# Attention into a gated MLP on one core: GpSimd's order, the sinks' keys, beta's turns and the fillers of the opening

## The chip, the cores and the metric

The kernel runs on one core of one Trainium2 chip. The metric is the device time of one execution in microseconds, median over runs. TensorE (PE) multiplies, ScalarE (ACT) evaluates exp and tanh, VectorE (DVE) masks, normalises and gates, GpSimd (POOL) casts, makes masks and issues transfers, SyncE (SP) issues transfers.

## The reference

```
attention: scores = q k^T / 8 over 768 positions, D = 64, 4 batches x 8 heads
           kept where k_pos < 4 (sinks) or 0 <= q_pos - k_pos < 128; softmax; times v
x    = attention output as [3072 tokens, 512]
h    = x @ w_in            (512 x 2048)
g    = h * sigmoid(beta*h) (beta: one value for each of the 2048 columns)
out  = g @ w_out           (2048 x 512), float32
```

## The kernel before

The 3072 tokens are eight tiles of 384 (half of a batch's 768 positions). Attention works on 32 units: a unit `n` is one tile and one pair of heads, four units to a tile. For a unit, q and k are cast to bf16, turned by TensorE (`transpose_first` for the first four, `transpose_in` for eight more, a transposing transfer for the rest), multiplied to scores, exponentiated by ScalarE into `E`, multiplied with v and a column of ones (`attend`), divided by VectorE (`normalise`) into `o_norm`, and turned again into `xT`. The first four units have their window mask added on TensorE: two products of `ident` with `add_mask` (the mask preloads, L711) stand ahead of each half of a unit's scores (L722).

Then, for each tile, 16 hidden blocks `h = w_in^T xT` (L836, four products each), tanh on ScalarE (L844, scaled by `beta_half`), the gate on VectorE (L857), and the output products with `w_out` (L865), interleaved with the attention of later tiles.

`Prog` is a planner. `op` records operations with what they read and write; `order` and `round` place them engine by engine from estimated costs; `emit` writes each engine's program in that order, with a semaphore wait wherever a dependency is not already implied. `after=[...]` adds a dependency that is only there to hold an operation back; between two operations of one engine it can become a wait of the engine for its own earlier instruction. `seq="name"` puts operations of one list into a fixed order without a semaphore. The planner also sets fillers on TensorE: until the hidden products of the first tile, it puts products of ones with ones (L461, into `acc[0]`, which nobody reads then) into a gap that it foresees, 0.8 of the gap less 60 ns, with a filler's cost doubled before `WARM` = 7000 ns.

The loads of the opening: SyncE issues q and k of the first four units, each 192 KB (`load_qk`), ScalarE issues beta and the first v (`load_v32`). GpSimd casts k and v (`cast`, L634; `cast_v`, L543) and issues w_in in four parts (`load_w_in`, L590); the first four keys of each head, the sinks, come by two small transfers from GpSimd's queue that also cast them to bf16 (`load_sinks(1, ...)`, L605, into `k_rows`), are turned by `sink_keys` (L617) and copied into `k_sink`. SyncE's second round of q and k (units 4 to 7) is held until w_in's second part has landed. beta arrives as 16 rows of 128; four fp32 turns on TensorE (L941) and four small VectorE operations (L946) make `beta_half`, just ahead of the last turns into `xT`.

Of the kernel before, what the change touches and what calls it, by code (L numbers as in the profile page):

```python
# [106 lines left out]
class Prog:  # L107
# [13 lines left out]
    QUEUE = {"sp": 1200.0, "act": 1200.0, "gp": 2100.0}  # L121
    TAIL, MIX, HEAVY, RING = 900.0, 1.1, 2.5, 8

    WARM, SWITCH = 7000.0, 95.0

    def __init__(self):
        self.nodes = []
# [114 lines left out]
    def round(self, took, freed):  # L242
        for n in self.nodes:
            n.open, n.place, n.ready = len(n.preds), None, 0.0
        free = dict.fromkeys(self.ENGINES, self.BEGIN)
        left = {e: [n for n in self.nodes if n.eng == e] for e in self.ENGINES}
        head = dict.fromkeys(self.ENGINES, 0)
        can = {e: [n for n in left[e] if n.open == 0] for e in self.ENGINES}
        issued = dict.fromkeys(self.ENGINES, 0)
        mode = 128  # L250
        placed = []

        def best(e):
# [12 lines left out]
            n = min(c, key=lambda n: (at[n.id], n.id))  # L266
            return at[n.id], n

        while any(n.place is None for n in self.nodes):
            found = [(*b, e) for e in self.ENGINES if (b := best(e)) is not None]  # L270
            start, n, e = min(found, key=lambda f: (f[0], f[1].id))
            busy = n.busy
            if e == "pe":
                if self.filler is not None and self.fill_until.place is None:
                    fn, cost, (source, _) = self.filler
                    at = max(free[e], source.done) if source.place is not None else start
                    cost *= 2.0 if at < self.WARM else 1.0
                    for _ in range(int((start - at - 60.0) * 0.8 / cost)):
                        f = Node(-1, "pe")
                        f.items.append((fn, None, [self.filler[2]]))  # L280
                        f.place = at
                        placed.append(f)
                        at += cost
                if n.mode != mode:
                    start, mode = start + self.SWITCH, n.mode
                if start < self.WARM:
                    busy *= 2.0
            free[e] = start + busy
            if n.dma is None:
                n.done = start + busy + n.lag  # L290
            else:
                n.done = start + took.get(n.id, busy + n.work + 3000.0)
                issued[e] += 1
            n.place = start
            can[e].remove(n)
            placed.append(n)
            for s in n.succs:
                s.open -= 1
                soft = n.id not in s.hard or (s.eng == e and n.dma is None)
                s.ready = max(s.ready, start + busy if soft else n.done)  # L300
                if s.open == 0:
                    can[s.eng].append(s)
        return placed
# [64 lines left out]
def bass_streamingllm_window__then__act_swish_beta_kernel(  # L368
# [45 lines left out]
    qk16 = [sb(f"qk16_{z}", (128, 2, 3, 2, D), BF16) for z in range(NQK)]  # L414
    v_aug = sb("v_aug", (128, 4, 2, 7, D + 2), BF16)
    v_sink = sb("v_sink", (128, NPAIR, 2, D1), BF16)
    k_rows = sb("k_rows", (NPAIR, NSINK, 2, D), BF16)
    k_sink = sb("k_sink", (128, NPAIR, 128), BF16)
    qkT = [sb(f"qkT{z}", (128, 2, 2, TT), BF16) for z in range(4)]
    E = [sb(f"E{z}", (128, 2, 768), BF16) for z in range(NE)]  # L420
# [121 lines left out]
    def cast_v(n):  # L542
        op("gp", lambda e: e.tensor_copy(v_aug[:, n, :, 0:3, 0:D].rearrange("p h c d -> p c h d"),  # L543
                                         v_stage[:, :, 2 * n:2 * n + 2, :]),
           r=[("v_stage", n // 2, c) for c in range(3)],
           w=[("v", n, kb, hh) for kb in range(3) for hh in range(2)], busy=460.0, lag=100.0)

    def load_v(T, c, after=()):

# [35 lines left out]
    w_in_src = moe_w_in.rearrange("(c p) f -> p c f", p=128)  # L585
    w_out_src = moe_w_out.rearrange("(g p j) n -> p g j n", p=128, j=PER)

    def load_w_in(m, ms, after=()):
        here = slice(m * 128, (m + ms) * 128)
        op("gp", lambda e: e.dma_start(w_in16[:, :, here], w_in_src[:, :, here]), after=after,  # L590
           w=[("w_in", c, mm) for c in range(4) for mm in range(m, m + ms)],
           dma=f"wi{m}", late=0.0 if m else 800.0, **transfer(DM * ms * 128 * 4, 385, 740.0, 3.0))

# [6 lines left out]
    def load_sinks(x, after=()):  # L600
        for hh in range(2):
            rows = slice(HEAD1 * hh, HEAD1 * hh + NSINK)
            if x:
                src = k[:, :, 0:NSINK, :].rearrange("b (g h) s d -> h (b g) s d", h=2)[hh]
                op("gp", lambda e, hh=hh, src=src: e.dma_start(k_rows[:, :, hh, :], src),  # L605
                   w=[("k_rows", hh)], after=after, dma=f"sk{hh}", busy=650.0, lag=300.0, weight=0.4)
            else:
                src = v[:, :, 0:NSINK, :].rearrange("b (g h) s d -> s h (b g) d", h=2)[:, hh]
                op("gp", lambda e, rows=rows, hh=hh, src=src: e.dma_start(v_sink[rows, :, hh, 0:D], src),
                   w=[("v_sink", hh)], r=["v_sink"], after=after, dma=f"sv{hh}", busy=650.0, lag=400.0, weight=0.4)  # L610

    def sink_keys():

        bank16 = tr_ps[:, :].bitcast(BF16)
        with P.together("pe"):
            for s in range(NSINK):
                op("pe", lambda e, s=s: nc.tensor.transpose(  # L617
                    bank16[:, s * NPAIR:(s + 1) * NPAIR],
                    k_rows[:, s, :, :].rearrange("n h d -> n (h d)"), ident[0:NPAIR, 0:NPAIR]),
                   r=[("k_rows", 0), ("k_rows", 1), "ident"], w=["tr"], **pe(60))  # L620
        src = bank16[:, 0:NSINK * NPAIR].rearrange("x (s n) -> x n s", s=NSINK)
        for hh in range(2):
            rows = slice(64 * hh, 64 * hh + 64)
            op("act", lambda e, hh=hh, rows=rows: e.copy(
                k_sink[rows, :, HEAD1 * hh:HEAD1 * hh + NSINK], src[rows]),
               x=["tr"], r=["k_sink"], w=[("k_sink", hh)], **act(100))

    def cast(n):
        _, _, half, pb = place(n)
        z = n % NQK  # L630
        here = slice(3 * half, 3 * half + 3)
        for x, name in enumerate("qk"):
            eng = "dve" if n < 4 and x == 0 else "gp"
            op(eng, lambda e, x=x, name=name, eng=eng: (e.copy if eng == "act" else e.tensor_copy)(  # L634
                qk16[z][:, x, :, :, :], stage[name][pb][:, :, here, :].rearrange("p h c d -> p c h d")),
               r=[(name + "_stage", pb, half)], w=[(name + "16", z)],
               **(dve(300.0) if eng == "dve" else {"busy": 460.0, "lag": 100.0}))

    def aside(n, step):
# [248 lines left out]
    for n in range(4):  # L888
        for x in range(2):
            load_qk(n, x)  # L890
    for c in range(6):
        load_v32(c // 3, c % 3)
    op("act", lambda e: e.activation(scratch[:, :], ones32[:, 0:1], AF.Exp, bias=0.0, scale=1.0),
# [1 line left out]
    cast(0)  # L895
    cast(1)
    cast_v(0)
    load_w_in(0, 4, [("v", 0, 0, 0)])
    cast_v(1)
    cast(2)  # L900
    load_sinks(1, [("v", 1, 0, 0)])

    select(ident32[:, :], ones32[:, :], [[1, 32]], ALU.is_equal, 0.0, 0, -1, ["ones32"], ["ident32"])
    transpose_first(0)
# [4 lines left out]
            scores(n, c, pairs[c])  # L909

    transpose_first(1)
    first_scores(0)
    cast(3)
    load_w_in(4, 4, [("k16", 0)])
    cast_v(2)
    load_w_in(8, 4, [("v", 2, 0, 0)])
    cast_v(3)
    load_w_in(12, 4, [("v", 3, 0, 0)])
    for n in range(4):
        if n < 2:  # L920
            transpose_first(n + 2)
        if n < 3:
            first_scores(n + 1)
        if n == 2:
# [5 lines left out]
            load_sinks(0, [("v", 3, 0, 0)])  # L930
# [8 lines left out]
    with P.together("pe"):  # L939
# [4 lines left out]
    with P.together("dve"):  # L944
        for y in range(PER):
# [1 line left out]
                beta_half[32 * y:32 * y + 32, :].rearrange("p (g j) -> p j g", j=PER),  # L947
                acc[1][0:32, 0:PER * NM].rearrange("p (j g y) -> p j g y", j=PER, y=PER)[:, :, :, y],
                0.5, None, ALU.mult),
               x=["acc1"], w=["beta"], **dve(100.0))  # L950
# [124 lines left out]
```

## Time and profile before

| | us |
|---|---|
| median of 3 runs (226.69 to 227.7) | 226.96 |
| the profiled execution | 228.2 |
| its span, first to last instruction | 226.5 |
| PE busy | 220.2 |
| ACT busy | 140.8 |
| DVE busy | 132.4 |
| POOL busy | 123.7 |

A busy PE counts pipelined matmuls whose ends are modelled. In the lists below, a row has its start, its length, the engine, the line, the operation, and in brackets how long the engine had been idle before it and what ended that. PEld is TensorE's weight load, and an engine with a q behind it (SPq, POOLq) is its issuing of transfers. In the chain of work in order of time a row is start, length, engine, tile and line. q0 is the transfer queue that GpSimd's issues go to, q1 SyncE's, q10 ScalarE's.

### The profile page before, as it was taken

The page shows a single profiled execution, that of the slowest core. Times are in us where ns is not written, and L with a number is a line of the kernel's source. Part 1 is how long each engine was busy: PE and PEld are TensorE (multiplying, and loading weights), DVE is VectorE, ACT ScalarE, POOL GpSimd, SP SyncE. Part 2 cuts the span into 40 slices and gives each one's busy share as a digit, 9 for nine tenths or more (in the row PEclk, how much of TensorE's full clock was granted, in tenths as well). Part 3 has the DMA queues.
Part 4 walks back from the last instruction along what each step waited for, and adds up shares of the span by engine and source line. Part 5 has one row for each costly group of instructions (what it writes and reads, how often), then busy time and mean ns, then how long its engine had stood idle before and what let it go on. Part 6 is the DMA issues. An engine that isn't in the chain of part 4 may idle for free.

```text
span 226.5 us, 4467 instructions
## 1 busy us (share of the span) xinstructions
PE 220.2 (97%) x1764; PEld 131.2 (58%) x1764; DVE 132.4 (58%) x263; ACT 140.8 (62%) x220; POOL 123.7 (55%) x191
## 2 busy tenths in 40 slices
PE   7999988999999999999999999999999999999995
PEld 4557654565666565555555555555565555555554
DVE  5447887549886666656565555566566555443300
ACT  1576887349576687656776766656676773555410
POOL 4589791989967969793939578694500000000000
PEclk9999999999999999999999999999999999999999
DMA  6999999999999999999999999999912202111022
GB/s 173 252 157 159 263 213 209 252 223 162 143 140 77 117 145 158 136 135 145 127 106 133 132 110 147 129 101 162 124 36 64 67 17 64 49 46 46 13 82 93
DMA packets 95877, 28.92 MB, mean 128 GB/s; under 512 B 83424, under 2 KB 91888, under 8 KB 95856
## 3 DMA queue, kind: packets, MB, share of 16 engines
q0 software_dynamic: 58208, 10.92, 61.5%
q1 hardware_dynamic: 34304, 16.79, 32.7%
q10 hardware_dynamic: 3344, 0.93, 1.9%
q8 instruction: 14, 0.23, 0.4%
q14 instruction: 7, 0.06, 0.1%
HBM read 27.34 MB, written 6.29 MB: 148 GB/s over the span
## 4 chain that ended last, share of the span: by engine, by line
PE 92%; ACT 3%; DMA 2%; SPq 0%; DVE 0%; issue 0%; ACTq 0%
PE acc L865 36%; PE h_ps L836 34%; PE s_ps L749 5%; PE s_ps L792 4%; DMA q_stage<-in_q_dram 2%; PE acc L836 2%; PE h_ps L865 2%; PE acc L792 1%; ACT E L729 1%; PE s_ps L781 1%; PE s_ps L692 1%; PE acc L461 1%; PE s_ps L711 1%; PE s_ps L722 1%; PE s_ps L674 1%; ACT th L844 1%
## 5 line engine op out<-in xcount | busy, mean ns | idle before, releaser
L844 ACT ACTIVATE th<-h_ps,beta_half 128x384 f32<-128x384 f32 x120 | 69.1, 581 | 53.0 <-PE h_ps L836 52.1
L865 PE MATMUL acc<-w_out,g 128*128 128x512 bf16 x368 | 99.4, 380 | 0.0
L836 PE MATMUL h_ps<-xT,w_in 128*128 128x384 bf16 x480 | 96.1, 326 | 0.0
L857 DVE SCALAR_TENSOR_TENSOR g<-th,h_ps 128x384 bf16<-128x384 f32 x120 | 65.5, 550 | 45.0 <-ACT th L844 44.3
L836 PEld LDWEIGHTS h_ps<-xT,w_in 128*128 128x128 bf16 x480 | 53.0, 113 | 33.7 <-DVE g L857 1.0
L865 PEld LDWEIGHTS acc<-w_out,g 128*128 128x128 bf16 x368 | 33.0, 98 | 27.9 <-issue 3.5
L564 POOL DMA_DIRECT2D land<-in_q_dram x40 | 30.2, 760 | 24.5 <-DVE rden L801 24.4
L757 ACT ACTIVATE E<-s_ps 128x1536 bf16<-128x1536 f32 x24 | 34.7, 1444 | 2.2 <-PE s_ps L749 2.1
L763 DVE TENSOR_TENSOR E<-E,mask 128x1536 bf16<-128x1536 bf16 x24 | 23.0, 957 | 15.8 <-ACT E L757 15.7
L564 POOL DMA_DIRECT2D land<-in_k_dram x40 | 30.3, 761 | 0.0
L573 POOL DMA_DIRECT2D v_aug<-in_v_dram x40 | 30.3, 761 | 0.0
L873 ACT ACTIVATE out_sb<-acc 128x512 f32<-128x512 f32 x23 | 13.7, 598 | 12.0 <-PE acc L865 11.8
L792 PEld LDWEIGHTS s_ps<-v_aug,E 128*128 128x128 bf16 x288 | 13.2, 97 | 2.9 <-issue 1.3
L792 PE MATMUL s_ps<-v_aug,E 128*128 128x65 bf16 x288 | 14.6, 193 | 0.0
L803 DVE TENSOR_TENSOR o_norm<-s_ps,rden 128x384 bf16<-128x384 f32 x24 | 13.3, 556 | 0.8
L749 PE MATMUL s_ps<-qkT 64*128 64x128 bf16 (+2 forms) x168 | 12.1, 257 | 0.0
L749 PEld LDWEIGHTS s_ps<-qkT 64*128 64x128 bf16 x168 | 5.7, 94 | 8.2 <-issue 6.2
L729 ACT ACTIVATE E<-s_ps 128x768 bf16<-128x768 f32 x9 | 7.3, 822 | 4.9 <-PE s_ps L722 4.9
L781 PE MATMUL s_ps<-v_sink,E_sink 128*128 128x130 bf16 x48 | 9.3, 219 | 0.0
L634 POOL CAST qk<-k_stage 128x384 bf16<-128x384 f32 x12 | 6.2, 513 | 5.2 <-DMA k_stage<-in_k_dram 5.2
L695 ACT ACTIVATE E_sink<-s_ps 128x384 bf16<-128x384 f32 x16 | 7.9, 493 | 0.8 <-PE s_ps L692 0.8
L554 POOL DMA_DIRECT2D v_aug<-in_v_dram x6 | 5.3, 898 | 5.1 <-DMA w_out<-in_moe_w_out_dram 5.1
(81 smaller groups left out, 159.6 us busy)
## 6 DMA issues: line engine op xcount, KB each, us to landing
out_dram<-out_sb SPq DMA_DIRECT2D x23, 256.0 KB, 2.4
q_stage<-in_q_dram SPq DMA_DIRECT2D x12, 192.0 KB, 6.9
k_stage<-in_k_dram SPq DMA_DIRECT2D x12, 192.0 KB, 7.2
w_in<-in_moe_w_in_dram POOLq DMA_DIRECT2D x4, 512.0 KB, 8.4
w_out<-in_moe_w_out_dram POOLq DMA_DIRECT2D x8, 256.0 KB, 8.8
land<-in_q_dram POOLq DMA_DIRECT2D x40, 48.0 KB, 3.1
land<-in_k_dram POOLq DMA_DIRECT2D x40, 48.0 KB, 3.6
v_aug<-in_v_dram POOLq DMA_DIRECT2D x40, 48.0 KB, 3.5
```

What stands on the lines that cost most here:

```text
L564: op("gp", lambda e, d=d, s=s: e.dma_start(d, s), w=[("land", pb, half, x, hh)], after=after, late=1800.0, dma=f"l{pb}{half}{x}{hh}", **tr ...
L573: op("gp", lambda e, d=d, s=s: e.dma_start(d, s), w=[("v", pb, 3 * half + c, hh) for c in range(3)], after=after, dma=f"lv{pb}{half}{hh}", ...
L749: op("pe", lambda e, at=at, w=w, kb=kb, qb=qb, nq=nq, hh=hh, rows=rows, bank=bank: e.matmul(s_ps[:, 2 * hh + bank, at:at + w], keys_of(pb, ...
L757: op("act", lambda e: e.activation(E[z][:, :, :], src, AF.Exp, bias=0.0, scale=SCALE), x=list(S_NAMES), w=[("E", z, 0), ("E", z, 1)], **ac ...
L763: op("dve", lambda e: e.tensor_tensor(E[z][:, :, :], E[z][:, :, :], m.unsqueeze(1).to_broadcast([128, 2, 768]), ALU.mult), r=[("E", z, 0), ...
L792: last=(x == len(kbs) - 1): e.matmul(av_ps[:, at + hh * D1:at + hh * D1 + D1], E[z][:, hh, col:col + 128], v_aug[:, pb, hh, column(n, kb), ...
L803: op("dve", lambda e: e.tensor_tensor(o_norm[o][:, :, :, :].rearrange("p m h d -> p (m h) d"), src[:, :, 0:D], rden[z][:, :].unsqueeze(2). ...
L836: op("pe", lambda e: e.matmul(bank, w_in16[:, c, m // PER * 512 + m % PER:m // PER * 512 + 512:PER], xT[:, c, T * TT:(T + 1) * TT], start= ...
L844: op("act", lambda e: e.activation(th[i % 3][:, :], bank, AF.Tanh, bias=0.0, scale=beta_half[:, m:m + 1]), x=[name], r=["beta"], w=[("th", ...
L857: op("dve", lambda e: e.scalar_tensor_tensor(g[T % 2][:, m, :], th[i % 3][:, :], 1.0, bank, ALU.add, ALU.mult), r=[("th", i % 3)], x=[name ...
L865: op("pe", lambda e: e.matmul(bank[:, 0:width], g[T % 2][:, m, t * 128:(t + 1) * 128], w_out16[:, m, cols], start=(m == 0), stop=(m == NM ...
L873: op("act", lambda e: e.activation(out_sb[z][:, 0:width], bank[:, 0:width], AF.Copy, bias=0.0, scale=0.5), x=[name], w=[("out_sb", z)], ** ...
```

## The change

- GpSimd: the casts of the first four units, the casts of v and the four issues of w_in are put on one list (`seq="loads gp"`), and the `after` that held w_in's parts behind casts goes. The third k is cast ahead of the second v.
- The sinks' keys: `k_rows` becomes fp32 and is loaded by two issues on SyncE, behind its first eight; `sink_keys` turns fp32 with `ident32`.
- beta's turns are recorded ahead of the first scores, and VectorE's part of it behind the cast of unit 1's q. In the resulting order TensorE's four turns stand right behind the first fillers, ahead of the first mask preloads.
- The fillers' rule has three stages: before 7 us the whole gap, to 10 us 0.8 of the gap less 60 ns at 1.5 times the cost, later half of the gap less 200 ns; the count is rounded at 0.7. TensorE's fillers in order are 14, 3, 5, 3, 7, 1, 2, 2, 3, 1, 7 before and 18, 3, 8, 2, 5, 1, 3 after.

Since the planner places everything anew, other instructions move too: between about 35 and 60 us some scores and output products on TensorE change places; the first is the second half of unit 7's scores, which goes from ahead of the first output products to behind the eighth.

```diff
-    WARM, SWITCH = 7000.0, 95.0
+    WARM, SURE, SWITCH = 7000.0, 10000.0, 95.0
...
-                    cost *= 2.0 if at < self.WARM else 1.0
-                    for _ in range(int((start - at - 60.0) * 0.8 / cost)):
+                    cost *= 2.0 if at < self.WARM else 1.5 if at < self.SURE else 1.0
+                    gap = start - at if at < self.WARM else 0.8 * (start - at - 60.0) if at < self.SURE else 0.5 * (start - at - 200.0)
+                    for _ in range(int(gap / cost + 0.3)):
...
-    k_rows = sb("k_rows", (NPAIR, NSINK, 2, D), BF16)
+    k_rows = sb("k_rows", (NPAIR, NSINK, 2, D), F32)
...  cast_v:
-           w=[("v", n, kb, hh) for kb in range(3) for hh in range(2)], busy=460.0, lag=100.0)
+           w=[("v", n, kb, hh) for kb in range(3) for hh in range(2)], busy=460.0, lag=100.0, seq="loads gp")
...  load_w_in:
-        op("gp", lambda e: e.dma_start(w_in16[:, :, here], w_in_src[:, :, here]), after=after,
+        op("gp", lambda e: e.dma_start(w_in16[:, :, here], w_in_src[:, :, here]), seq="loads gp",
...
+    def load_sink_keys():
+        for hh in range(2):
+            src = k[:, :, 0:NSINK, :].rearrange("b (g h) s d -> h (b g) s d", h=2)[hh]
+            op("sp", lambda e, hh=hh, src=src: e.dma_start(k_rows[:, :, hh, :], src),
+               w=[("k_rows", hh)], dma=f"sk{hh}", seq="loads sp", busy=520.0, lag=150.0, weight=0.4)
...  sink_keys:
-                    k_rows[:, s, :, :].rearrange("n h d -> n (h d)"), ident[0:NPAIR, 0:NPAIR]),
+                    k_rows[:, s, :, :].rearrange("n h d -> n (h d)"), ident32[0:NPAIR, 0:NPAIR]),
...  cast:
+               seq="loads gp" if eng == "gp" and n < 4 else None,
...  main program:
+    load_sink_keys()
...
-    load_w_in(0, 4, [("v", 0, 0, 0)])
-    cast_v(1)
-    cast(2)
-    load_sinks(1, [("v", 1, 0, 0)])
+    load_w_in(0, 4)
+    cast(2)
+    cast_v(1)
...  moved from behind the loop over the first four units to ahead of first_scores(0):
+    with P.together("pe"):
+        for j in range(PER):
+            op("pe", ... nc.tensor.transpose(acc[1][0:32, j * NM:(j + 1) * NM], beta_stage[:, j:128:PER], ident32[0:NM, 0:NM]) ...)
+    with P.together("dve"):
+        for y in range(PER):
+            op("dve", ... x=["acc1"], w=["beta"], after=[("q16", 1)], **dve(100.0))
...
-    load_w_in(4, 4, [("k16", 0)])
+    load_w_in(4, 4)
-    load_w_in(8, 4, [("v", 2, 0, 0)])
+    load_w_in(8, 4)
-    load_w_in(12, 4, [("v", 3, 0, 0)])
+    load_w_in(12, 4)
```

More of the change, by code (lines that the diff above doesn't have):

```diff
@@ L586, in bass_streamingllm_window__then__act_swish_beta_kernel, with load_w_in @@
     w_out_src = moe_w_out.rearrange("(g p j) n -> p g j n", p=128, j=PER)
-    def load_w_in(m, ms, after=()):
+    def load_w_in(m, ms):
         here = slice(m * 128, (m + ms) * 128)
-        op("gp", lambda e: e.dma_start(w_in16[:, :, here], w_in_src[:, :, here]), after=after,
+        op("gp", lambda e: e.dma_start(w_in16[:, :, here], w_in_src[:, :, here]), seq="loads gp",
            w=[("w_in", c, mm) for c in range(4) for mm in range(m, m + ms)],
@@ L598, in load_w_out, with load_sinks @@
            dma=f"wo{m}", **transfer(ms * 128 * NOUT * 4, 416, 740.0, 3.0))
-    def load_sinks(x, after=()):
+    def load_sink_keys():
[3 more added lines that the diff above has]
+               w=[("k_rows", hh)], dma=f"sk{hh}", seq="loads sp", busy=520.0, lag=150.0, weight=0.4)
+    def load_sinks(after=()):
         for hh in range(2):
             rows = slice(HEAD1 * hh, HEAD1 * hh + NSINK)
[L603 to L610, printed above, removed]
+            src = v[:, :, 0:NSINK, :].rearrange("b (g h) s d -> s h (b g) d", h=2)[:, hh]
+            op("gp", lambda e, rows=rows, hh=hh, src=src: e.dma_start(v_sink[rows, :, hh, 0:D], src),
+               w=[("v_sink", hh)], r=["v_sink"], after=after, dma=f"sv{hh}", busy=650.0, lag=400.0, weight=0.4)
     def sink_keys():
-        bank16 = tr_ps[:, :].bitcast(BF16)
         with P.together("pe"):
@@ L617, in sink_keys @@
                 op("pe", lambda e, s=s: nc.tensor.transpose(
-                    bank16[:, s * NPAIR:(s + 1) * NPAIR],
-                    k_rows[:, s, :, :].rearrange("n h d -> n (h d)"), ident[0:NPAIR, 0:NPAIR]),
-                   r=[("k_rows", 0), ("k_rows", 1), "ident"], w=["tr"], **pe(60))
-        src = bank16[:, 0:NSINK * NPAIR].rearrange("x (s n) -> x n s", s=NSINK)
+                    tr_ps[:, s * NPAIR:(s + 1) * NPAIR],
+                    k_rows[:, s, :, :].rearrange("n h d -> n (h d)"), ident32[0:NPAIR, 0:NPAIR]),
+                   r=[("k_rows", 0), ("k_rows", 1), "ident32"], w=["tr"], **pe(60))
+        src = tr_ps[:, 0:NSINK * NPAIR].rearrange("x (s n) -> x n s", s=NSINK)
         for hh in range(2):
@@ L911, in bass_streamingllm_window__then__act_swish_beta_kernel @@
     transpose_first(1)
+    with P.together("pe"):
+        for j in range(PER):
+            op("pe", lambda e, j=j: nc.tensor.transpose(acc[1][0:32, j * NM:(j + 1) * NM], beta_stage[:, j:128:PER],
+                                                        ident32[0:NM, 0:NM]),
+               r=["beta_stage", "ident32"], w=["acc1"], **pe(64))
+    with P.together("dve"):
+        for y in range(PER):
+            op("dve", lambda e, y=y: e.tensor_scalar(
+                beta_half[32 * y:32 * y + 32, :].rearrange("p (g j) -> p j g", j=PER),
+                acc[1][0:32, 0:PER * NM].rearrange("p (j g y) -> p j g y", j=PER, y=PER)[:, :, :, y],
+                0.5, None, ALU.mult),
+               x=["acc1"], w=["beta"], after=[("q16", 1)], **dve(100.0))
     first_scores(0)
     cast(3)
-    load_w_in(4, 4, [("k16", 0)])
+    load_w_in(4, 4)
     cast_v(2)
-    load_w_in(8, 4, [("v", 2, 0, 0)])
+    load_w_in(8, 4)
     cast_v(3)
-    load_w_in(12, 4, [("v", 3, 0, 0)])
+    load_w_in(12, 4)
     for n in range(4):
@@ L929, in bass_streamingllm_window__then__act_swish_beta_kernel @@
             masks([("v", 3, 0, 0)])
[L930 removed]
+            load_sinks([("v", 3, 0, 0)])
             for c in range(3):
@@ L936, in bass_streamingllm_window__then__act_swish_beta_kernel @@
         normalise(n, *bank)
-    with P.together("pe"):
-        for j in range(PER):
-            op("pe", lambda e, j=j: nc.tensor.transpose(acc[1][0:32, j * NM:(j + 1) * NM], beta_stage[:, j:128:PER],
-                                                        ident32[0:NM, 0:NM]),
-               r=["beta_stage", "ident32"], w=["acc1"], **pe(64))
-    with P.together("dve"):
-        for y in range(PER):
-            op("dve", lambda e, y=y: e.tensor_scalar(
[L947 to L950, printed above, removed]
     for n in range(4):
```

## The prediction

> **What bounds the kernel now.** I read the page's 40 slices first, then its chain of work that ended last, then that chain in order of time for 0 to 60 us.
>
> ```profile
> PE   7999988999999999999999999999999999999995
> PEclk9999999999999999999999999999999999999999
> PE 92%; ACT 3%; DMA 2%; SPq 0%; DVE 0%; issue 0%; ACTq 0%
> 8.29 0.43 PE acc L461 x3
> 8.72 0.32 PE s_ps L674 x3
> 9.04 0.64 PE s_ps L711 x2
> 9.68 0.75 PE acc L461 x7
> 12.94 0.33 PE s_ps L711 x2
> 15.23 0.11 PE acc L461 x2
> 17.61 0.17 PE acc L461 x3
> 18.44 0.14 PE acc L941 x4
> 18.91 0.39 PE acc L461 x7
> 19.30 0.26 PE s_ps L820 x3
> 19.55 0.49 PE h_ps L836 x3
> 28.24 0.34 PE s_ps L656 x3
> 36.24 0.34 PE h_ps L722 x4
> 36.58 0.97 PE acc L865 x4
> 38.42 0.86 PE acc L865 x4
> ```
>
> TensorE (PE) carries 92% of the chain, and from 37 us on nothing else stands in it. The work behind that point is the same in both kernels, so this case is decided by what TensorE loses before. It loses at three places: the opening up to the first hidden product at 19.55, the turns of the second round of q and k at 28.24, and the stretch before 36.24, where ScalarE paces.
>
> Two more things are in these rows. The L461 rows are fillers: products of ones that nobody reads, put where the planner expects TensorE to wait. They are on the chain themselves, so a filler in the wrong place delays the work behind it. And two mask preloads took 0.64 us at 9.04 but 0.33 us at 12.94: TensorE worked at half rate until about 12.8 us, although the granted clock reads full in every slice.
>
> **The fillers.** In the changed program's order the first gaps get 18, 3 and 8 fillers instead of 14, 3 and 5; the next two get 2 and 5 instead of 3 and 7; all later ones together get 4 instead of 16.
>
> ```profile
> 1.16 1.68 PE L461 MATMUL acc<-ones 128*128 128x128 bf16 x14 [1.16 <-DVE ones L455]
> 4.71 0.50 PE L674 MATMUL s_ps<-ident,qk 128*128 128x128 bf16 x3 [0.47 <-DVE qk L634]
> 4.94 0.51 POOL L634 CAST qk<-k_stage 128x384 bf16<-128x384 f32 x1 [1.98 <-DMA k_stage<-in_k_dram]
> 6.75 0.50 PE L722 MATMUL s_ps<-qkT 64*128 64x384 bf16 x2 [0.21 <-DVE qkT L681]
> 16.14 1.51 ACT L729 ACTIVATE E<-s_ps 128x768 bf16<-128x768 f32 x2 [0.16 <-PE s_ps L722]
> 18.52 0.56 DVE L803 TENSOR_TENSOR o_norm<-h_ps,rden 128x384 bf16<-128x384 f32 x1
> ```
>
> A cold filler costs 0.75 / 7 = 0.107 us. The 18 first ones end at 1.16 + 18 x 0.107 = 3.09. Then come beta's four turns (0.14 at full rate, up to 4 x 0.107 = 0.43 cold) and four preloads at 0.32 each, together 1.28: 4.5 to 4.8 against the 4.71 at which q's first turn starts anyway. A slip of 0.1 would end at the next wait, because k's turn needs the cast that ends at 4.94 + 0.51 = 5.45. The eight fillers behind it start at about 5.82 (k's turn at 5.50 plus 0.32) and end at 6.68, before the scores at 6.75. The added fillers are hidden, by hundredths.
>
> The removed ones are worth more. From 8.29 to 12.94 the chain is TensorE alone, without a wait, so three cold fillers fewer there bring 3 x 0.107 = 0.32. Behind 12.94 TensorE and ScalarE's exponentials release each other in turn, which keeps this lead but adds little. The last exponential ends at 16.14 + 1.51 = 17.65, and three fillers stand in front of the product that waits for it (17.61); one is left, which brings 2 x 0.056 = 0.11. The last turn needs o_norm, ready at 18.52 + 0.56 = 19.08, and starts at 19.30 behind seven fillers; three are left, and of these 0.22 us I take 0.1 (the rest is the hop between the engines). Sum of the opening: 0.53. Its bounds are 0, if the exponentials and copies were late by themselves, and 1.0, if every filler from 12.94 on counted: 12 fewer at 0.056 are 0.67 beside the 0.32.
>
> **Beta's turns.**
>
> ```profile
> 0.81 0.43 ACTq L886 DMA_DIRECT2D beta_stage<-in_moe_beta_dram  x1
> beta_stage<-in_moe_beta_dram ACTq DMA_DIRECT2D x1, 8.0 KB, 2.2
> 9.08 0.56 DVE L681 COPY qkT<-s_ps 128x384 bf16<-128x384 bf16 x1 [1.79 <-PE s_ps L674]
> 19.00 0.73 DVE L946 TENSOR_SCALAR beta_half<-acc 32x16 f32<-32x16 f32 x4
> ```
>
> They leave 0.14 us of TensorE at 18.44 and 0.73 us of VectorE at 19.00. At 18.44 TensorE was early for o_norm anyway. VectorE's work, ending at 19.73, held the last xT copy by 0.2 us (its turn ended at 19.30 + 0.26), and six hidden products at 0.49 / 3 each, 19.55 to 20.53, cover that copy. So this brings nothing. In the new place VectorE's 0.73 lies in an idle 1.79 us ahead of 9.08; without that cover it would cost its 0.73. TensorE's four turns add a wait for beta's transfer, landing at 0.81 + 2.2 = 3.01, just ahead of the 3.09 at which they are reached. The preloads and q's first turn are queued behind it, with VectorE and ScalarE waiting for them; a landing up to 0.3 later would be swallowed, and each us beyond costs at most one. I take 0.
>
> **GpSimd's waits and the sinks' keys.**
>
> ```profile
> POOL w_in L590 <- POOL v_aug L543: 0.9, 3, 0.3
> 11.00 1.02 POOL L605 DMA_DIRECT2D k_rows<-in_k_dram  x2
> 12.82 0.76 POOL L590 DMA_DIRECT2D w_in<-in_moe_w_in_dram  x1 [0.30 <-POOL qk L634]
> 4.62 0.47 SPq L533 DMA_DIRECT2D k_stage<-in_k_dram  x1
> k_stage<-in_k_dram SPq DMA_DIRECT2D x1, 192.0 KB, 7.2
> q0 software_dynamic: 208, 0.21, 125.3%
> q0 software_dynamic: 211, 0.06, 106.9%
> w_in<-in_moe_w_in_dram POOLq DMA_DIRECT2D x1, 512.0 KB, 7.9
> 20.73 0.37 SPq L533 DMA_DIRECT2D q_stage<-in_q_dram  x1
> 27.67 0.51 POOL L634 CAST qk<-k_stage 128x384 bf16<-128x384 f32 x1 [0.37 <-DMA k_stage<-in_k_dram]
> ```
>
> GpSimd waited for itself 0.9 + 0.3 us ahead of w_in's four issues and spent 1.02 us on issuing k_rows. Both go. The next bound is the last k transfer of the first round: issued at 4.62, landed at 11.82, cast by 12.36. So w_in's second part is issued at 12.36 instead of 12.82. The two q0 rows are the software queue in 13 to 14 us and in 14 to 15 us: with k_rows' small packets it moved 0.06 MB instead of 0.21, about 0.7 us lost, and this goes too. The second part then lands 0.5 to 1.2 us before its 12.82 + 7.9 = 20.72; I take 1.0, nearer the end where issue and k_rows both count. SyncE starts the second round of q and k on this landing (20.73). That round's first k is cast at 27.67 and turned at 28.24, so the 0.53 us from the opening pass this point. Without this part TensorE would stand there, and the opening's gain would be lost.
>
> On SyncE the two moved issues (about 0.47 each) run from 5.1 to 6.1, where nothing is queued until 20.73. Their 16 KB lie behind k's last transfer and are due just ahead of beta's old place at 18.44. Their fp32 turns and copies are the same in number; I take 0, within 0.1 either way.
>
> **A reordered score.**
>
> ```profile
> 36.24 0.34 PE L722 MATMUL h_ps<-qkT 64*128 64x128 bf16 x4 [0.36 <-ACT E L729]
> ```
>
> In the changed order the first eight output products stand ahead of this score instead of behind it, so TensorE does not wait these 0.36 us for ScalarE. The score then stands alone among full-height products, and the change of tile shape is paid once more: 0.97 - 0.86 = 0.11. Net 0.25, between 0 and 0.36. The products need w_out up to 0.7 us sooner; w_out's issues follow GpSimd's, 0.7 to 1.0 earlier.
>
> **Sum.** 0.53 + 0.25 = 0.78, say 0.8. The profiled execution took 228.2 us, 1.7 more than its span of 226.5, and would take 227.4. The median of the three runs is 226.96; less 0.8, that is **226.2 us**.
>
> **The rivals.** *Full rate comes earlier.* Before, TensorE waits 0.47 us ahead of 4.71 and 0.21 ahead of 6.75; the new fillers close these. If the half rate ended near 9.4 instead of 12.8, the chain's 9.04 to 12.94 would shrink by up to 3.9 x 0.48 = 1.9 us (0.48 is 1 - 0.33 / 0.64). The second round's turns at 28.24 can follow by 1.0 only. With the score's 0.25 that is 1.25: 225.7. For it: the stretch that preceded full rate was the first one without a wait. Against it: the stretch before holds twelve turns of q and k, and nothing here shows whether these count. The Trainium skill (TensorE: Matmul & The Clock Gate, Part 1) has the array at half rate until it was busy through one window of about 3.4 us, whose phase is free; by that rule the closed gaps give this rival's 225.7, and the trace's late step at 12.8 agrees with it. The same page (Part 4) says that transposes do not count as busy in the same way; by that the early window would still fail and 226.2 stand.
>
> *The opening's gain is given back at 28 us*, if w_in's second part lands no sooner because the transfers themselves fill the queue (125.3% of it): only 0.25 stays, 226.7. *The change does nothing*: fillers only stood in waits for data, and the score's wait comes back behind the next exponential: 226.95.
>
> *Full rate comes later.* The 26 fillers from 8.29 on become 11, and gaps open there. Each us of half rate beyond 12.8 costs 0.48 us, so 0.78 / 0.48 = 1.6 us more turns the gain into a loss. If it takes one more stretch as long as 9.04 to 12.94, that is 3.9 x 0.48 = 1.9, and 226.96 - 0.78 + 1.9 = 228.1. Against it: of the removed fillers most stood behind 12.94.
>
> **How the numbers follow.** 226.2: 0.38. Early full rate, 225.7: 0.34. Given back, 226.7: 0.10. Nothing, 226.95: 0.06. Late full rate, 228.1: 0.12. The range of 225.2 to 227.4 takes in the unknown sizes of the first two (0.5 to 1.5 us of gain, and 0.25 for the spread of runs) and the small cases above; it leaves out the late case and a little on either side. About 0.5%, 1.13 us, is what a measurement of this kernel can tell from no change: below 225.83 lie two thirds of the early case and a quarter of the main one, 0.33 in all; above 228.1 about half of the late case and odd ones such as a late beta, 0.10; the rest is 0.57.
>
> **What would show it.** Right: the first hidden product near 19.0, no wait on TensorE for beta, w_in's second part landing before 20.2, no TensorE wait ahead of the second round's turns or of the moved score. Mask preloads of 0.33 before 10 us would mean the early case. Wrong: preloads of 0.64 after 13 us, or a TensorE wait at about 28 us for a cast.

## The result and the profile after

The changed kernel takes 226.40 us, median of 17 runs (225.87 to 228.03). The kernel before, in 17 runs on the same chip, takes 227.65 (226.69 to 229.06). The ratio is 0.9958, with a 95% interval of 0.9938 to 0.9978: a gain of 0.2 to 0.6%. That is 1.25 us in the medians and about 0.95 us by the ratio, which is an estimate of its own and not the quotient of the medians. Executions well above the rest of their kernel, four of before and one each of e3 and e6 below, are left out of the ratios. The profiled execution of after took 226.34 us with a span of 224.6.

The page of after, its busy slices of TensorE, the granted clock and the chain by engine:

```profile
PE   7899979999999999999999999999999999999995
PEclk9999999999999999999999999999999999999999
PE 90%; ACT 4%; DMA 2%; DVE 1%; SPq 1%; issue 1%; POOL 0%; ACTq 0%
```

TensorE has fallen from 92% to 90% of the chain. Its own busy time fell too, from 220.2 to 218.1 us. Eight fillers fewer can't be more than 8 x 0.107 = 0.86 of these 2.1 us, so some of the rest ran faster. The granted clock reads full in every slice, as it did before, so this row can't show it. TensorE's instructions in order of time can (start, length, engine, line, operation, and the wait before it):

```profile
3.43 0.82 PE L713 MATMUL s_ps<-add_mask,ident 128*128 128x384 bf16 x2
4.71 0.51 PE L676 MATMUL s_ps<-ident,qk 128*128 128x128 bf16 x3
5.79 0.77 PE L462 MATMUL acc<-ones 128*128 128x128 bf16 x8
6.74 0.34 PE L724 MATMUL s_ps<-qkT 64*128 64x384 bf16 x2 [0.18 <-DVE qkT L683]
...
8.64 0.49 PE L713 MATMUL s_ps<-add_mask,ident 128*128 128x384 bf16 x2
```

The rows of before to set beside them:

```profile
5.80 0.74 PE L461 MATMUL acc<-ones 128*128 128x128 bf16 x5
...
8.84 0.85 PE L711 MATMUL s_ps<-add_mask,ident 128*128 128x384 bf16 x2
...
12.78 0.49 PE L711 MATMUL s_ps<-add_mask,ident 128*128 128x384 bf16 x2
```

The first scores took 0.50 us at 6.75 before and take 0.34 at 6.74 here. The start is the same and the length is that of full rate. The eight fillers at 5.79 take 0.77, hardly more than five took before (0.74 at 5.80): the step to full rate lies within them. Before, it lay near 12.8 us. The preloads of before took 0.85 us at 8.84; here they take 0.49 at 8.64 (a pair is longer in this list than in the chain, where it has 0.64 at half rate and 0.33 at full).

The chain of after in order of time:

```profile
17.99 0.49 PE acc L838 x3
...
26.50 0.34 PE s_ps L658 x6
...
34.13 0.97 PE acc L867 x4
```

The first hidden products stand at 17.99 instead of 19.55, the turns of the second round at 26.50 instead of 28.24, the first output products at 34.13 instead of 36.58. Nothing waits ahead of the moved score, and no cast of the second round is late. The second part of w_in came earlier by more than that. The first row is the list of transfers for 12 to 13.2 us (KB each, us to landing), the second SyncE's issues:

```profile
w_in<-in_moe_w_in_dram POOLq DMA_DIRECT2D x1, 512.0 KB, 5.6
```
```profile
18.16 0.38 SPq L534 DMA_DIRECT2D q_stage<-in_q_dram  x1
```

The second part of w_in, issued at 12.58, took 5.6 us instead of 7.9. SyncE starts the second round of q and k on its landing, at 18.16 instead of 20.73.

### The profile page after: what moved, and what is told of

Read it like the earlier page. It is cut to its first block, busy times and chain, and to the rows that moved or that the text cites. A ratio compares the mean times of both kernels' runs of the same rounds, so it can differ in the third digit from the quotient of the medians.

```text
span 224.6 us, 4452 instructions
## 1 busy us (share of the span) xinstructions
PE 218.1 (97%) x1756; PEld 129.9 (58%) x1756; DVE 132.1 (59%) x263; ACT 140.5 (63%) x220; POOL 122.7 (55%) x189
## 4 chain that ended last, share of the span: by engine, by line
PE 90%; ACT 4%; DMA 2%; DVE 1%; SPq 1%; issue 1%; POOL 0%; ACTq 0%
PE acc L867 37%; PE h_ps L838 35%; PE s_ps L751 5%; PE s_ps L794 4%; DMA k_stage<-in_k_dram 2%; PE acc L838 2%; ACT E L731 2%; PE h_ps L867 2%; PE s_ps L783 1%; PE s_ps L694 1%; PE acc L794 1%; PE s_ps L724 1%; ACT th L846 1%; SPq L534 1%; ACT qkT L665 1%; PE acc L658 1%
## 5 line engine op out<-in xcount | busy, mean ns | idle before, releaser
L794 PEld LDWEIGHTS s_ps<-v_aug,E 128*128 128x128 bf16 x288 | 13.2, 97 | 2.9 <-issue 1.3
```

Source lines behind the costliest of these rows:

```text
L794: last=(x == len(kbs) - 1): e.matmul(av_ps[:, at + hh * D1:at + hh * D1 + D1], E[z][:, hh, col:col + 128], v_aug[:, pb, hh, column(n, kb), ...
```

## The experiments

Two numbers of a profile carry most of what follows: where the first hidden product starts, and the rest, which is the span less that start. The first tells what the opening did, the second whether TensorE was kept fed behind it. All starts are taken from one view, the instructions that read w_in (in the chain above the same product stands 0.1 to 0.2 us later). A kernel's "step" is where, in its one profile, the first scores or preloads wholly at full rate start.

| kernel | median, us | ratio to before, 95% interval | step | first product | span | rest |
|---|---|---|---|---|---|---|
| before | 227.65 | 1 | 12.8 | 19.4 | 226.5 | 207.1 |
| after | 226.40 | 0.9958 [0.9938, 0.9978] | 6.74 | 17.8 | 224.6 | 206.8 |
| e1 early fillers as before | 227.09 | 0.9963 [0.9931, 0.9995] | 6.78, lost, 12.5 | 18.7 | 225.5 | 206.8 |
| e2 later fillers as before | 226.37 | 0.9955 [0.9929, 0.9981] | 6.62 | 17.2 | 224.0 | 206.8 |
| e3 no fillers | 227.48 | 0.9984 [0.9955, 1.0012] | 14.14 | 19.9 | 226.7 | 206.8 |
| e4 before, gaps filled | 228.21 | 1.0012 [0.9986, 1.0039] | 6.73 | 17.6 | 226.6 | 209.0 |
| e5 the four waits back | 227.74 | 0.9994 [0.9966, 1.0022] | 7.57 | 17.3 | 225.2 | 207.9 |
| e6 keys on GpSimd again | 226.24 | 0.9947 [0.9917, 0.9977] | 7.51 | 17.4 | 224.4 | 207.0 |
| e7 the score back | 226.65 | 0.9961 [0.9934, 0.9989] | 6.81 | 18.1 | 225.3 | 207.2 |
| e9 fillers in every gap | 226.38 | 0.9944 [0.9914, 0.9974] | 6.71 | 17.8 | 224.6 | 206.8 |
| e10 before, no waits | 227.18 | 0.9992 [0.9966, 1.0018] | 9.73 | 17.9 | 225.8 | 207.9 |
| e11 before, no waits, gaps filled | 226.28 | 0.9957 [0.9929, 0.9985] | 6.97 | 18.3 | 225.2 | 206.9 |
| e12 GpSimd delayed | 226.96 | 0.9978 [0.9953, 1.0002] | 6.78 | 17.3 | 226.0 | 208.7 |
| e8 beta back | 227.00 | 0.9971 [0.9941, 1.0000] | 6.80 | 17.3 | 224.1 | 206.8 |

e1 to e12 have 10 to 12 runs each. The kernel before was run 35 times beside each of the three groups (e1 to e4; e5 to e9; e10 to e12 with e8) and took 227.71, 227.63 and 227.56. These executions of before spread widely: of the 101 that are in the ratios, 30 took less than 227.0 us and 31 took 228.0 or more. Its profile, at 228.2, is one of the upper third; where the step lies in the lower third no profile shows. In the diffs a list of fillers gives their number in each gap, in TensorE's order. In e1 to e12, e8 aside, the order of all other instructions is the planner's, and only what the diff shows is changed.

### e1: the early fillers as before

```diff
-fillers 18, 3, 8, 2, 5, 1, 3
+fillers 14, 3, 5, 2, 5, 1, 3
```

> The changed kernel with the first gaps filled as before (14, 3, 5 instead of 18, 3, 8); order and all else kept. Clock theory: full rate comes about 3 us later than in the changed kernel, so mask preloads near 8.8 us take about 0.64 us a pair instead of 0.33, the first hidden product starts at 18.8 to 19.1 instead of 17.99, and the time is 0.7 to 1.1 us longer than the changed kernel's. Chance theory (the step to full rate falls where it falls, whatever the fillers): no difference in time beyond 0.3 us.

TensorE's instructions in e1's profile:

```profile
6.78 0.34 PE L742 MATMUL s_ps<-qkT 64*128 64x384 bf16 x2 [0.46 <-ACT qkT L701]
8.82 0.85 PE L731 MATMUL s_ps<-add_mask,ident 128*128 128x384 bf16 x2
12.50 0.49 PE L731 MATMUL s_ps<-add_mask,ident 128*128 128x384 bf16 x2
```

The same profile by stretches (start and end, length, then the busy time of PE, PEld, DVE, ACT and POOL with their numbers of instructions, then the granted clock, DMA share and GB/s):

```profile
8.00:10.00 2.00, 1.47 (x10) 1.08 (x10) 0.93 (x2) 1.05 (x2) 1.90 (x4) 0.59 1.18 286
10.00:12.00 2.00, 2.00 (x15) 0.83 (x14) 0.64 (x2) 1.06 (x2) 0.86 (x2) 0.56 1.02 176
12.00:14.00 2.00, 2.00 (x33) 1.32 (x31) 1.22 (x3) 1.61 (x4) 1.94 (x4) 1.00 1.16 192
```

Here full rate came early as well, although the gaps were open, and was lost again: the granted clock reads 0.59 and 0.56 from 8 to 12 us, and the preloads at 8.82 are back at 0.85. The first product came 0.9 us later than in after, and the rest is the same 206.8. So in this one profile the old early fillers allowed the step but did not hold it. The median is 0.7 us above after's, but the ratio of 0.9963 is close to after's 0.9958 and the intervals overlap: what the added early fillers are worth in after is not shown by the times.

### e2, e3 and e9: how many fillers, and where

```diff
e2
-fillers 18, 3, 8, 2, 5, 1, 3
+fillers 18, 3, 8, 3, 7, 1, 2, 2, 3, 1, 7
e3
-fillers 18, 3, 8, 2, 5, 1, 3
+no fillers
e9
-fillers 18, 3, 8, 2, 5, 1, 3
+fillers 18, 3, 8, 4, 3, 7, 1, 2, 2, 1, 3
```

> The changed kernel with the later fillers as before (3, 7, 1, 2, 2, 3, 1, 7 instead of 2, 5, 1, 3), the first gaps as changed. Clock theory: full rate still comes near 6.5 us; the 19 more fillers cost 0.056 us each where they stand on the chain, so the first hidden product comes 0.2 to 0.6 us later. Filler theory (the removed later fillers are the gain): it comes back to 18.8 or later, 0.8 to 1.0 us lost.

> The changed kernel without any filler. Clock theory: full rate comes later than in any other kernel, beyond 12.8 us, the first hidden product at 19.5 to 21, the time 1.5 to 3 us above the changed kernel's. Chance theory: fillers only cost, so it is as fast as the changed kernel or 0.2 us faster.

> The changed kernel with more fillers: 4 ahead of unit 1's q turn, 3 instead of 2 ahead of its k turn, 7 instead of 5 ahead of its scores, and 1, 2, 2 in the gaps behind. Clock theory (gaps near 7 and 8 us can take full rate away again): full rate is held in every run from its first step on, no run with a granted clock below 1.00, median 0.2 to 0.5 us below the changed kernel's. Rival (fillers on the chain cost): 0.1 to 0.4 us slower.

e2 has all of before's later fillers and takes 226.37, e9 has some more ahead of the later turns and takes 226.38: the same as after within 0.03 us, and the same rest. The fillers that the change took out cost nothing that can be measured where they stood. Without any fillers (e3) TensorE's list shows a long wait and a late step:

```profile
7.81 0.50 PE L742 MATMUL s_ps<-qkT 64*128 64x384 bf16 x2 [1.69 <-ACT qkT L701]
...
13.25 0.85 PE L731 MATMUL s_ps<-add_mask,ident 128*128 128x384 bf16 x2
...
14.14 0.49 PE L731 MATMUL h_ps<-add_mask,ident 128*128 128x384 bf16 x2
```

The first scores wait 1.69 us, half rate lasts until about 14, the first product stands at 19.9, and the median is 227.48, though the interval of its ratio still overlaps that of after.

### e4: the kernel before, with only its early gaps filled

```diff
-fillers 14, 3, 5, 3, 7, 1, 2, 2, 3, 1, 7
+fillers 14, 4, 3, 8, 3, 7, 1, 2, 2, 3, 1, 7
```

> The kernel before with the first gaps filled and nothing else: 4 fillers between the mask preloads and q's first turn, 8 instead of 5 ahead of the first scores. Clock theory: full rate comes at 6 to 9.5 us, the first hidden product at 18.0 to 18.8, and most of the gain is there: 0.7 to 1.2 us faster than the kernel before, unless w_in's second part, which lands as late as before, holds TensorE at 28 us (supply theory: then at most 0.3 us faster, with a wait of 0.5 to 1 us ahead of the second round's turns).

The opening did what after's does: scores at full rate at 6.73, first product at 17.6, 1.8 us earlier than before. And the time did not fall: 228.21. TensorE's instructions with their waits in e4's profile:

```profile
21.00 0.84 PE L854 MATMUL acc<-xT,w_in 128*128 128x384 bf16 x4 [0.62 <-DMA w_in<-in_moe_w_in_dram]
26.55 0.84 PE L854 MATMUL acc<-xT,w_in 128*128 128x384 bf16 x4 [0.16 <-DMA w_in<-in_moe_w_in_dram]
27.99 0.34 PE L674 MATMUL s_ps<-ident,qk 128*128 128x128 bf16 x3 [0.29 <-POOL qk L652]
...
34.10 0.34 PE L674 MATMUL s_ps<-ident,qk 128*128 128x128 bf16 x3 [0.49 <-POOL qk L652]
```

And the first issue of SyncE's second round there:

```profile
20.97 0.37 SPq L551 DMA_DIRECT2D q_stage<-in_q_dram  x1
```

TensorE now stands for w_in at 21.00, just behind the landing of its second part at 20.97, as late as before. It stands for a later part at 26.55, and at 27.99 and 34.10 for the casts of the second round, whose loads start on that landing. The four waits are 1.56 us. The rest grew from 207.1 to 209.0 us, by 1.9: all of the 1.8 was given back. This is what the prediction named as the bound behind the opening.

### e5: after, with the four waits of GpSimd put back

```diff
 w_in part 1, 2, 3, 4 (GpSimd's order as in after)
+wait for GpSimd's own cast ahead: v of unit 0, k of unit 3, v of unit 2, v of unit 3
```

> The changed kernel with GpSimd's four waits for its own casts ahead of w_in's issues put back; order, queues and fillers kept. Supply theory (what counts is when w_in's second part and the second round of q and k land): the second part is issued about 0.3 us later (near 12.9) and lands near 18.5 instead of 18.16, still ahead of its use near 20.6, so no wait on TensorE and no difference in time beyond 0.2 us. Rival (the waits themselves are the gain): 0.9 to 1.2 us slower than the changed kernel.

The second w_in issue in GpSimd's list of e5's profile:

```profile
12.37 0.74 POOL L612 DMA_DIRECT2D w_in<-in_moe_w_in_dram  x1 [0.31 <-POOL qk L657]
```

And the first output product in TensorE's list:

```profile
34.69 1.04 PE L889 MATMUL acc<-w_out,g 128*128 128x512 bf16 x4 [0.65 <-DMA w_out<-in_moe_w_out_dram]
```

The same product in after:

```profile
34.06 1.04 PE L867 MATMUL acc<-w_out,g 128*128 128x512 bf16 x4
```

Each wait takes some 0.3 us, and GpSimd's last w_in issue stands at 15.47 instead of 14.94, its first w_out issue at 24.79 instead of 24.22. In this profile w_in's second part was not late (SyncE's second round starts at 17.97). What was late is w_out: TensorE waits 0.65 us for it at the first output products. In after the product starts without a wait. The median is 227.74: the gain over before is gone, and even the lowest of the twelve, 226.77, is above the medians of after, e6, e7 and e9. So the removed waits count. By the one profile, which at 226.99 is among e5's shorter executions, they do so through the later issues of GpSimd's line, and not only through the one part that the prediction had followed.

### e6: after, with the sinks' keys on GpSimd's queue

```diff
-k_rows fp32, two issues on SyncE behind its first eight
+k_rows bf16, two issues on GpSimd ahead of the fourth k cast, as before
```

> The changed kernel with the sinks' keys back on GpSimd's queue, cast to bf16 by the transfer, issued ahead of w_in's second part; all else kept. Supply theory: w_in's second part lands 1 to 2.5 us later (19.2 to 20.7); where full rate comes early TensorE waits up to 0.6 us for it near 20.6 and up to 1 us for the casts of the second round near 27, and the time is 0.3 to 1.2 us above the changed kernel's. Rival (the queue had room): no difference beyond 0.2 us.

SyncE's second round in e6's profile:

```profile
17.74 0.37 SPq L560 DMA_DIRECT2D q_stage<-in_q_dram  x1
```

226.24 us. The second part of w_in landed as early as in after, with the small packets of k_rows in front of it. Moving the keys brought nothing that these times show.

### e7: after, with the moved score put back

```diff
-eight output products, second half of unit 7's scores
+second half of unit 7's scores, eight output products
```

> The changed kernel with the second half of unit 7's scores put back ahead of the first output products; all else kept. Order theory: TensorE waits 0.36 us for ScalarE ahead of this score again, and the span less the start of the first hidden product is 206.95 as in the kernel before, instead of 206.6; the time is 0.25 to 0.36 us longer. Rival (the wait only moves): 206.6 and no difference.

The score in its old place, in TensorE's list of e7's profile:

```profile
34.78 0.34 PE L748 MATMUL h_ps<-qkT 64*128 64x128 bf16 x4 [0.36 <-ACT E L757]
```

The wait for ScalarE's exponential is back, 0.36 us, and the rest is 207.2 instead of 206.8. The median is 0.25 us higher, too little to be measured by itself. Nor is the rest a proof: e11 below has the score in its old place with the same wait of 0.36, and a rest of 206.9.

### e10 and e11: the kernel before without its waits, and with both

```diff
e10 (before)
-GpSimd waits for its own casts ahead of the four w_in issues
e11 (e10)
-fillers 14, 3, 5, 3, 7, 1, 2, 2, 3, 1, 7
+fillers 14, 4, 3, 8, 3, 7, 1, 2, 2, 3, 1, 7
```

> The kernel before with one thing done: GpSimd no longer waits for its own casts ahead of the four w_in issues; its order, the keys on its queue, the fillers and the scores stay as before. Theory (the gain needs an early full rate of TensorE and earlier loads together): here TensorE still reaches full rate near 12.8 us and begins the hidden products near 19.5 us, where the weights of before were in time but for 0.36 us, so 227.2 to 227.7 us, span less hidden start 206.6 to 207.0. Rival (the loads alone bring the gain): 226.4 to 226.8 us.

> The kernel before with two things done: the four waits ahead of the w_in issues taken away, and the 4 and 3 fillers added ahead of the second transposes and the first scores. Theory (both are needed): first hidden product near 17.6 us, no wait of TensorE for w_in or w_out, span less hidden start 207.0; 226.5 to 226.9 us, that is the time of after with the moved score's 0.25 to 0.35 us left out. Rival (the fillers' gain is lost to something else than the four waits: the keys on GpSimd's queue together with the rest of the old order): 227.5 to 228.2 us as with the fillers alone, with TensorE waiting for w_in at 21 us.

The four kernels with and without each part are the main result. With the waits and without the fillers 227.65, with the fillers alone 228.21 (ratio 1.0012 [0.9986, 1.0039]), without the waits alone 227.18 (0.9992 [0.9966, 1.0018]), both together 226.28 (0.9957 [0.9929, 0.9985]). Neither part alone makes a difference that can be measured; the two together give the whole of after's 0.9958. The interval of both lies clear of that of the fillers alone; it overlaps that of the waits alone. e11, seven fillers and four waits away from before, is the smallest edit that gives after's time; no kernel here beats it by more than its uncertainty.

The profiles were not where they had been expected. e10 has the opening of before, instruction for instruction on TensorE, but its step came at 9.73 instead of 12.8, and its first product at 17.9:

```profile
9.73 0.34 PE L745 MATMUL s_ps<-qkT 64*128 64x384 bf16 x2
```

So with the gaps open the step varies for reasons that are not in the program: 9.73, 12.8, 14.14 without fillers, and in e1 early and lost again. With them filled it came by 7.6 us in all ten profiles. That the fillers act through this rests on these profiles, one of each kernel, rather than on the times. e10's rest of 207.9 is another matter: TensorE was at half rate once more, later. The stretches of e10's profile (columns as in e1):

```profile
30.00:32.00 2.00, 1.20 (x16) 0.56 (x14) 1.30 (x3) 2.00 (x4) 1.78 (x5) 1.00 1.59 205
32.00:33.00 1.00, 0.68 (x9) 0.41 (x9) 0.96 (x3) 1.00 (x3) 1.00 (x3) 1.00 1.17 211
33.00:34.00 1.00, 1.00 (x14) 0.70 (x14) 0.52 (x1) 1.00 (x3) 0.45 (x1) 0.52 1.12 211
34.00:35.00 1.00, 1.00 (x18) 0.71 (x15) 0.36 (x2) 0.72 (x2) 0.00 (x0) 0.50 1.10 205
35.00:36.00 1.00, 0.67 (x7) 0.28 (x3) 0.97 (x3) 0.95 (x2) 0.00 (x0) 0.50 1.16 215
36.00:37.00 1.00, 1.00 (x7) 0.51 (x6) 0.86 (x2) 0.56 (x1) 0.00 (x0) 0.77 1.10 205
```

e11's profiled execution, at 226.93, was one of the longer ones of its twelve; its first product stood at 18.3, and its rest of 206.9 shows no wait for weights.

### e12: after, with GpSimd delayed without a wait

```diff
 (GpSimd, ahead of w_in part 2)
+memset of one half of k_sink, set again later as before
```

> The kernel after with one thing added: a MEMSET of half of k_sink (some 0.9 us) on GpSimd ahead of the second w_in issue, which delays all later loads of GpSimd by as much as the four waits did, without a semaphore wait; k_sink is set again later as before. Theory (what counts is when the loads are issued): 227.4 to 228.0 us, with TensorE waiting some 0.5 to 1.0 us for w_out near 34 us or for w_in near 21 us. Rival (the waits as such, or chance in the profiled run, made the kernel with the waits put back slow): 226.2 to 226.6 us, no wait for weights.

The median of 226.96 lies between the two expectations. The profiled execution is the longest of the twelve, 227.77. In it TensorE waits for the second round's casts (0.24 at 26.50 and the row below), and then loses its rate for 3.4 us as in e10:

```profile
30.38 0.69 PE L681 MATMUL s_ps<-ident,qk 128*128 128x128 bf16 x6 [0.58 <-POOL qk L658]
```

The granted clock in the same profile:

```profile
34.00:35.00 1.00, 0.99 (x14) 0.60 (x13) 0.37 (x2) 0.69 (x1) 0.00 (x0) 0.50 1.12 209
```

A delay of GpSimd does cost something by these rows, but e12 does not tell whether the waits of e5 cost more than the time that they take. It delays less than they do: GpSimd's first w_out issue stands at 24.58 here, at 24.79 in e5 and at 24.22 in after. The intervals of e5, e12 and after overlap in pairs.

### e8: after, with beta's turns in their old place

```diff
-beta's turns and halvings ahead of the first scores
+beta's turns and halvings behind the last normalisation, two fillers more in the second gap
```

> The kernel after with beta's turns and their four halvings on VectorE put back to where they stood, behind the last normalisation (2 fillers more in the place that they leave). Theory (beta's place is worth nothing, the four short VectorE operations are covered): 226.2 to 226.7 us, first hidden product near 18 us, no wait for beta. Rival (VectorE is late by their 0.4 us for the xT copies ahead of the hidden products): 226.7 to 227.0 us, hidden start 0.3 to 0.4 us later.

The median of 227.00 is 0.6 us above after's, the ratios' intervals overlap, and the profile, of one of the shortest executions of e8 (225.85), says the contrary: the first product at 17.3 and the rest at 206.8 are as good as any here. No wait for beta stands in it, nor in after. What beta's move is worth is left open, within about 0.6 us; no row shows a price.

## Why the prediction was right in its number, and wrong in its way

The forecast was 226.2 us in a range of 225.2 to 227.4, and 226.40 was measured. Two errors cancelled in it, by luck: it started from 226.96, the median of three runs, where 17 runs gave 227.65, and it counted a gain of 0.78 where 1.25 came.

*The fillers.* This step failed. It gave 0.53 us to the later fillers that were removed, and called the added early ones hidden. With the later ones back (e2) the time is the same, 226.37, so the 0.53 is not there. The added early ones go with the step: with both gaps filled, on the program of before or of after, ten profiles of ten reach full rate by 7.6 us and keep it through the opening; of the four with open gaps none does. The times bear this out only for the fillers and the loads together (e11); for the fillers alone they do not. What the prediction had as its first rival, with a chance of 0.34 and a gain of 1.25 us, is what the profile of after shows. That the medians differ by the same 1.25 is partly luck: the rival let the second round's turns follow by 1.0 only, and they came 1.74 earlier. The row that spoke for it was in the text: TensorE's waits of 0.47 and 0.21 ahead of 4.71 and 6.75. By the Trainium skill (TensorE: Matmul & The Clock Gate, Part 1) the array stays at half rate until it was busy through one window, of free phase. The ten profiles with both gaps filled, all at full rate from 7.6 us on at the latest, agree with this rule, and e10 against before fits the free phase: the same instructions, steps 9.73 and 12.8. The argument against the rival, that the turns of q and k in that stretch might not count as busy, did not decide it: the 3.4 us ahead of 6.74 in after hold six of them, and full rate came all the same.

*Beta's turns.* Taken as 0, and no row contradicts it; e8 is too uncertain to confirm it.

*GpSimd's waits and the keys.* The role of this step was right: without the waits the opening's gain passes. e4 shows the gain given back, and e11 shows it kept. Its working was partly wrong. The 0.7 us that k_rows' packets were to cost is not there (e6), and the landing of w_in's second part was put at 19.7 and came at 18.16, since the transfer took 5.6 us and not 7.9. What shortened it is not shown: it took 5.6 with the waits back (e5), 7.3 without them on the order of before (e10), 7.3 in e1 and 8.4 in e4, one profile each. And the bound was sought at the second round's turns alone, where e4 waited for w_in itself as well, and e5 for w_out.

*The reordered score.* Net 0.25 was forecast; putting it back cost 0.25 in the medians and 0.4 of the rest in the profile, with the wait of 0.36 in its old place. The rows agree with this step; its size is below what the times can show, and e11's rest speaks for less.

*The rivals.* The late full rate (228.1) did not come: with fewer fillers behind 8.29 the step was earlier, not later. The gain given back happened in e4, with the landing named there, but not in after.

## What to carry to other kernels

An opening and the loads behind it are one path: filling TensorE's early gaps and issuing the weights sooner were each worth nothing measurable alone and some 1.3 us together, so two changes that both measure as nothing may still be tried together. Where work ahead of the first long run of products may be at half rate, compare the lengths of equal instructions, not the granted clock, and try closing the short waits before it. And take the base of a forecast from many runs: three runs of this kernel were 0.7 us off, more than half of the effect.

## What the hardware showed that was not expected

TensorE lost full rate in places without any long wait. The single waits ahead of the loss were 0.26 to 0.41 us in e10 and 0.49 and 0.58 in e12, and around the loss 0.39 to 0.55 in e1. For each of the three, the stretch of 3.4 us ahead of the loss and the loss itself (e1, e10, e12; columns as in e1):

```profile
4.96:8.38 3.42, 2.14 (x25) 1.15 (x22) 1.72 (x6) 2.90 (x6) 0.93 (x2) 1.00 1.19 277
8.38:11.79 3.41, 3.26 (x21) 1.85 (x21) 1.57 (x3) 1.52 (x3) 2.38 (x5) 0.50 1.07 227
```
```profile
29.63:33.04 3.41, 2.27 (x27) 1.12 (x28) 2.58 (x6) 3.41 (x7) 3.16 (x8) 1.00 1.52 204
33.04:36.46 3.42, 3.08 (x29) 1.81 (x31) 2.26 (x5) 3.10 (x5) 0.41 (x1) 0.50 1.13 210
```
```profile
29.48:32.89 3.41, 2.22 (x24) 1.06 (x24) 2.33 (x4) 3.27 (x6) 3.41 (x8) 1.00 1.78 193
32.89:36.31 3.42, 3.02 (x26) 1.83 (x28) 2.25 (x6) 2.61 (x5) 0.72 (x2) 0.50 1.12 209
```

All three losses last 3.4 us at a granted clock of 0.50, and TensorE was busy for 63 to 67% of the 3.4 us ahead of them. That share alone does not decide: e7 was busy 1.20 of the 2.00 us from 30 to 32, as e10 was, and 2.14 of 3.42 from 4.10 to 7.52, and kept its rate. In the other profiles the stretch around 33 us passes at full rate too. The Trainium skill (TensorE: Matmul & The Clock Gate, Part 1) has the array go back to half rate after an idle window of about 3.4 us. These rows agree with the length, and disagree with an idle window as the condition, since no wait was near that long. The same part tells of another kernel in which frequent short idle times made the rate swing. The rows look like that.

Such a loss leaves a trace in an execution's mean granted clock, 0.992 in the profiles of e1, e10 and e12. A mean near that was seen in 23 of 105 executions of the kernel before, but in 6 of 89 executions of the kernels that have both the filled gaps and no waits (after, e2, e6, e7, e8, e9, e11); in these 89 the six have a median of 227.8 against 226.4 of the others. Counted by the fillers alone it was seen in 11 of 125 executions with both gaps filled and in 31 of 139 with them open. That the filled opening makes a loss rarer fits these counts, though e4, filled but with the waits, has three in twelve; why it should is not shown. It is not the whole gain: among the executions in the ratios with a mean of 0.999 or 1.00, before's median is 227.22 and after's 226.37.

Half rate at the start and half rate later look different in the record: the granted clock reads 1.00 through before's opening, whose preloads take twice their later time (0.64 against 0.33 in the chain), and 0.50 through the later losses.
